# Attention and a one-expert MoE on one core: the last transpose of a query tile is placed behind both heads' scores

## The chip, the cores and the metric

The kernel runs on one core of a Trainium2 chip. The metric is device time in microseconds (us). The kernel before takes 1197.86 us, the median of three runs from 1194.87 to 1198.07. Engines are named as in the profile: PE (TensorE; PEld are its weight loads), DVE (VectorE), ACT (ScalarE), POOL (GpSimd) and SP (SyncE, which here only issues DMAs).

## What is computed

Attention with 8 batches, 8 heads, 576 positions and head size 64, with a bias from a small network on relative positions, and behind it a mixture of experts in which each of the 4608 tokens goes to the one expert with the largest gate.

```python
scores = scale * np.matmul(q, k.transpose(0, 1, 3, 2)) + bias
scores = scores - np.max(scores, axis=-1, keepdims=True)
attn = np.exp(scores)
attn = attn / (np.sum(attn, axis=-1, keepdims=True) + 1e-09)
out = np.matmul(attn, v)                      # per batch and head
...
expert_idx = np.argmax(x @ w_gate, axis=1)
for e in range(E):
    mask = expert_idx == e
    h = np.maximum(x[mask] @ w1[e], 0.0)
    out[mask] = gate_w[mask, None] * (h @ w2[e])
```

## The kernel before

Two heads make a pair, and there are 32 pairs (8 batches of 4). The queries of a pair are cut into five tiles, four of 128 rows and one of 64. The first two pairs run while the bias is built (`attend`); the other thirty go through `attend_units`, which the change touches. There a unit is a pair with its tiles [0, 1] or [2, 3, 4] (the last two pairs have units of one tile), and a step `k` is one query tile.

For one step, `scores` writes the scores of the two heads into two PSUM tiles `s` (four matmuls each, line 165; the pool `ps_s` has two buffers). DVE adds the bias and takes the minimum of the negated scores (line 170), ACT takes the exponential (line 173). The result `a` has 128 queries by 1152 keys, so it needs nine transposes of 128 by 128 on PE before it can be multiplied with the values: `turn` writes four of them (block 0), four (block 1) and one (block 2, the one that holds the end of both heads' keys) into PSUM tiles `tps`. The pool `ps_t` has two buffers, which the blocks take in turn. Block 0 is copied out by ACT (line 216), block 1 by DVE (line 214), block 2 by ACT (line 206). For the 64-row tile the two heads lie side by side: there is no block 1, block 0 is copied by DVE (line 212), and block 2 (line 201) is copied by two ACT copies (line 203).

The steps are overlapped: while the scores of step k are written, blocks 0 and 1 of step k-1 are transposed (`first_turns`), block 2 belongs to step k-2 (`last_turn`), and a number of value products (lines 221 and 224) and output rows (line 234) of an older unit follow. On PE the order is the order in which the program writes these pieces, since each call of `pe` is tied behind the one before. On ACT, DVE, POOL and SP a scheduler sets the order from its own timeline of the whole program.

In one step PE therefore does: scores of head 1; block 2 of step k-2; scores of head 2; blocks 0 and 1 of step k-1; rows and value products. Because the two `tps` buffers alternate, block 1 of step k-1 takes the buffer that block 2 of step k-2 was written to, and has to wait until ACT has copied that out. After a 64-row tile there is no block 1, and so no such wait.

The q and k of a coming pair are loaded by SP into raw tiles (`qn`, `kn`, one buffer), split by ACT (line 139) and DVE (line 140) into a rounded part and a rest, and moved by DMAs of line 144 to `qs`, `k1` and `k2` (two buffers each). Once per batch, `route` ranks the tokens (lines 378 to 427): two small matmuls (lines 398 and 399), a chain of small DVE instructions up to the row numbers `pi` (line 411), and five indirect DMAs on POOL (line 425), which write the rows to DRAM. After attention the experts run (`Experts`), in blocks of up to 384 tokens.

Of the kernel before, what the change touches and what calls it, by code (L numbers as in the profile page):

```python
# [77 lines left out]
def attention(tc, ctx, q, kt, vm, ltab, bcst, gate, gt, cm, cmat, ival, tail0, pcst, bias, xs, plan, moe):  # L78
# [140 lines left out]
    def values(v, at, o, N):  # L219

        yield nc.tensor.matmul(o[:, :N], v[:, 4], at[:, 8, :N], start=True, stop=False, skip_group_check=True)
        for c in range(4):
            for hh in range(2):
                mm = nc.tensor.matmul(o[64 * hh:64 * hh + 64, :N], v[:, c, 64 * hh:64 * hh + 64], at[:, 4 * hh + c, :N], start=False, stop=c == 3, skip_group_check=True)  # L224
                if hh:
                    yield mm

    def rows(b, pr, qts, osb, rl):

        x = ps_x.tile([P, 512], F32, name="x")  # L230
        c0 = 0
        for i, qt in enumerate(qts):
            n = QN[qt]
            mm = nc.tensor.matmul(x[:n, i * XC:(i + 1) * XC], osb[:, c0:c0 + n], gt[:, pr], start=True, stop=True)
            c0 += n
        for i, (qt, r) in enumerate(zip(qts, rl)):
            n = QN[qt]
            if n < P:
                nc.vector.tensor_scalar(out=r[:, :1], in0=r[:, :1], scalar1=1e-9, scalar2=None, op0=ALU.add)
                nc.vector.reciprocal(out=r[:n, 1:2], in_=r[n:2 * n, :1])  # L240
                nc.vector.reciprocal(out=r[:n, :1], in_=r[:n, :1])
            else:
                nc.vector.tensor_scalar(out=r, in0=r, scalar1=1e-9, scalar2=None, op0=ALU.add)
                nc.vector.reciprocal(out=r, in_=r)
            rb = r[:n].rearrange("p (a o) -> p a o", o=1)
            nc.vector.tensor_tensor(out=xsb[b, qt][:n, pr * P:(pr + 1) * P].rearrange("p (a d) -> p a d", a=2),
                                    in0=x[:n, i * XC:i * XC + P].rearrange("p (a d) -> p a d", a=2), in1=rb.broadcast_to([n, 2, D]), op=ALU.mult)
            nc.vector.tensor_tensor(out=lgs[b % 2][:n, qt, pr], in0=x[:n, i * XC + P:(i + 1) * XC].rearrange("p (a e) -> p a e", a=2),
                                    in1=rb.broadcast_to([n, 2, E]), op=ALU.mult)
        return mm  # L250
# [15 lines left out]
    def attend_units(units, ahead, after):  # L266

        steps = [(u, i) for u, (b, pr, qts) in enumerate(units) for i in range(len(qts))]
        state = [{"a": [], "r": [], "N": 0} for _ in units]
        prev = []
        turned, ended, prod = [], [], []

        def pe(f):

            if prev:
                with tc.issue_after(prev[0].ins):
                    prev[:] = [f()]  # L280
            else:
                prev[:] = [f()]

        def finish():
            for u in ended:
                b, pr, qts = units[u]
                pe(lambda: rows(b, pr, qts, state[u]["osb"], state[u]["r"]))
                for qt in qts:
                    after(b, pr, qt)
            ended.clear()  # L290

        def products(count):

            for _ in range(count):
                if not prod:
                    if not turned:
                        return
                    u = turned.pop(0)
                    b, pr, qts = units[u]
                    o = ps_o.tile([P, 512], F32, name="o")  # L300
                    prod[:] = [u, 5, o, values(loaded[b * NPAIR + pr][3], state[u]["at"], o, state[u]["N"])]
                u, left, o, g = prod
                pe(lambda: next(g))
                prod[1] -= 1
                if not prod[1]:
                    prod.clear()
                    N = state[u]["N"]
                    state[u]["osb"] = atp[1].tile([P, atp[2]], F32, name="osb")
                    nc.scalar.copy(out=state[u]["osb"][:, :N], in_=o[:, :N])
                    ended.append(u)  # L310

        def first_turns(u, i):
            st, qts = state[u], units[u][2]
            if i == 0:
                while any("osb" not in st for st in state[:max(u - 1, 0)]):
                    products(1)
                st["at"] = atp[0].tile([P, 9, atp[2]], F32, name="at")
            pe(lambda: turn(st["a"][i], st["at"], QN[qts[i]], st["N"], [0, 1]))

        def last_turn(u, i):  # L320
            st, qts = state[u], units[u][2]
            pe(lambda: turn(st["a"][i], st["at"], QN[qts[i]], st["N"], [2]))
            st["N"] += QN[qts[i]]
            if i == len(qts) - 1:
                turned.append(u)

        extra = []

        def one_more():

            if extra:
                with tc.issue_after(prev[0].ins):
                    if next(extra[0], extra) is extra:
                        extra.clear()

        for k, (u, i) in enumerate(steps):
            b, pr, qts = units[u]
            more = ahead(b, pr, qts[i])
            if more:
                extra[:] = [more]  # L340
            one_more()
            halves = scores(b, pr, qts[i])
            pe(lambda: next(halves)[2])
            if k > 1:
                last_turn(*steps[k - 2])

            def second():
                a, r, mm = next(halves)
                state[u]["a"].append(a)
                state[u]["r"].append(r)  # L350
                return mm
            pe(second)
            if k:
                first_turns(*steps[k - 1])
                finish()
                products(UNIT_STEPS[(k - 1) % QT] if len(units[steps[k - 1][0]][2]) > 1 else 5)
        last_turn(*steps[-2])
        first_turns(*steps[-1])
        one_more()
        finish()  # L360
        products(5)
        one_more()
        last_turn(*steps[-1])
        one_more()
        products(10)
        mm = prev[0]
        finish()
        return mm
# [119 lines left out]
    with ExitStack() as es:  # L488
# [63 lines left out]
        steps = [(0, 0), (0, 1), (1, 0), (1, 1), (2, 0), (2, 1), (3, 0), (4, 0), (3, 1), (4, 1)]  # L552
# [36 lines left out]
    def after(b, pr, qt):  # L589
        advance(1)  # L590
        if pr == NPAIR - 1 and qt == QT - 1:
            pending.append(route(b))
# [312 lines left out]
```

## Time and profile before

| | |
|---|---|
| device time, median of 3 runs | 1197.86 us (1194.87 to 1198.07) |
| the profiled execution | 1203.04 us, of which the span of instructions 1201.3 us |
| mean granted TensorE clock | 0.965 |
| busy share of the span | PE 92%, PEld 74%, DVE 57%, ACT 46%, POOL 14% |
| PE busy from 300 to 450 us | 146.89 of 150 us |

Attention in `attend_units` runs from about 125 to 700 us, the experts from there to the end. The time of a row is its start from the span's start, then its length; a matmul's end is modelled, and matmuls overlap, so the pace of PE is read from the starts of neighbouring rows.

### The profile page before, as it was taken

How to read it: one execution, taken by the hardware profiler on the slowest of the kernel's cores; microseconds unless marked ns; L12 is line 12 of the kernel's file. 1: busy time of each engine (PE TensorE's matmuls, PEld its weight loads, DVE VectorE, ACT ScalarE, POOL GpSimd, SP SyncE). 2: the span in 40 equal slices, each digit the busy share in tenths (PEclk: the TensorE clock that was granted, in tenths of full speed). 3: DMA queues.
4: the chain of work that ended last, by engine and by line, in shares of the span. 5: the costliest groups of instructions: out<-in, count | busy, mean ns of one | idle time of the engine just before them, and what ended most of it. 6: DMA issues, size and time to landing. Idle time of an engine off the chain costs nothing. (4 is left out here: it accounts for less than half of the span.)

```text
span 1201.3 us, 21037 instructions
## 1 busy us (share of the span) xinstructions
PE 1111.0 (92%) x7332; PEld 883.0 (74%) x7332; DVE 680.7 (57%) x2025; ACT 558.3 (46%) x1315; POOL 168.6 (14%) x224
## 2 busy tenths in 40 slices
PE   6699889999999999999999997999989899989893
PEld 2256667777777777777677786998978788978782
DVE  6587667787787878878677763322413222414141
ACT  5587556676667666676566551111302211313130
POOL 0000000101001010010100402400042140032320
PEclk8699989999999999999999999999999999999897
DMA  8845765757658677576565705420251700342400
GB/s 227 191 117 119 186 154 156 208 162 206 164 157 215 160 203 181 153 217 173 174 171 159 229 34 183 187 71 27 71 186 45 251 27 18 102 155 71 168 18 27
DMA packets 70089, 171.85 MB, mean 143 GB/s; under 512 B 11298, under 2 KB 11810, under 8 KB 69794
## 3 DMA queue, kind: packets, MB, share of 16 engines
q1 hardware_dynamic: 63682, 150.07, 45.4%
q0 software_dynamic: 5920, 18.95, 4.3%
q8 instruction: 73, 1.20, 0.4%
q14 instruction: 126, 1.03, 0.3%
q10 hardware_dynamic: 288, 0.59, 0.1%
HBM read 75.00 MB, written 23.97 MB: 82 GB/s over the span
## 5 line engine op out<-in xcount | busy, mean ns | idle before, releaser
L165 PE MATMUL s<-k,qs 128*128 128x288 f32 x1280 | 238.9, 322 | 16.0 <-ACT ob L536 7.8
L173 ACT ACTIVATE a<-t,mn 128x576 f32<-128x576 f32 x288 | 222.7, 774 | 59.8 <-DVE mn L170 49.9
L165 PEld LDWEIGHTS s<-k,qs 128*128 128x128 f32 x1280 | 184.8, 191 | 75.6 <-issue 32.3
L693 PE MATMUL psh<-bias,bias 128*128 128x384 f32 (+2 forms) x1248 | 210.3, 326 | 23.6 <-issue 21.9
L170 DVE CUSTOM_DVE_ANT_0 t<-s,bias 128x576 f32<-128x576 f32 x288 | 210.8, 751 | 33.1 <-PE s L165 29.3
L693 PEld LDWEIGHTS psh<-bias,bias 128*128 128x128 f32 x1248 | 202.3, 198 | 29.8 <-issue 23.7
L210 PE MATMUL tps<-gt,a 128*128 128x128 f32 x1152 | 165.9, 278 | 15.3 <-ACT at L206 7.8
L683 ACT ACTIVATE bias<-psh 128x384 fp32r<-128x384 f32 (+2 forms) x104 | 46.7, 451 | 266.4 <-PE psh L693 266.1
L210 PEld LDWEIGHTS tps<-gt,a 128*128 128x128 f32 x1152 | 131.4, 142 | 35.8 <-ACT at L206 13.1
L224 PE MATMUL o<-at,v 128*64 128x320 f32 (+3 forms) x1216 | 154.3, 379 | 0.0
L684 DVE SCALAR_TENSOR_TENSOR bias<-psh,bias 128x384 fp32r<-128x384 f32 (+2 forms) x104 | 51.7, 504 | 112.2 <-ACT bias L683 111.9
L224 PEld LDWEIGHTS o<-at,v 128*64 128x64 f32 x1216 | 70.6, 136 | 51.2 <-issue 26.3
L214 DVE COPY at<-tps 128x512 f32<-128x512 f32 x128 | 87.9, 687 | 6.1 <-PE tps L210 1.6
L727 PE MATMUL psy<-w2h,bias 128*128 128x512 f32 (+1 forms) x224 | 88.8, 398 | 0.0
L216 ACT COPY at<-tps 128x512 f32<-128x512 f32 x128 | 73.9, 577 | 30.8 <-PE tps L210 30.2
L728 PE MATMUL psy<-w2l,bias 128*128 128x512 f32 (+1 forms) x224 | 88.2, 396 | 0.0
L729 PE MATMUL psy<-w2h,bias 128*128 128x512 f32 (+1 forms) x224 | 87.2, 397 | 0.0
L394 POOL TENSOR_TENSOR cs<-cs,oh 128x8 f32<-128x8 f32 x40 | 8.0, 201 | 512.8 <-DVE oh L389 510.4
L731 DVE TENSOR_SCALAR y<-psy,g 128x512 f32<-128x512 f32 (+1 forms) x38 | 28.4, 748 | 91.0 <-PE psy L729 91.0
L732 POOL DMA_INDIRECT out<-y,ids x38 | 37.2, 980 | 301.5 <-DVE y L731 269.1
L534 PE MATMUL s<-h,bc 128*32 128x288 f32 x576 | 59.2, 469 | 12.2 <-ACT ob L536 10.3
L668 ACT CAST bias<-tps 128x384 fp32r<-128x384 f32 (+2 forms) x60 | 24.9, 461 | 87.8 <-PE tps L666 78.4
(164 smaller groups left out, 1411.2 us busy)
## 6 DMA issues: line engine op xcount, KB each, us to landing
k<-hi SPq DMA_DIRECT2D x128, 160.0 KB, 2.9
k<-kn SPq DMA_DIRECT2D x128, 160.0 KB, 3.8
bias<-in_wl SPq DMA_DIRECT2D x28, 512.0 KB, 3.9
qn<-in_q SPq DMA_DIRECT2D x32, 352.0 KB, 4.1
qs<-hi SPq DMA_DIRECT2D x64, 176.0 KB, 2.9
qs<-qn SPq DMA_DIRECT2D x64, 176.0 KB, 3.2
kn<-in_kt SPq DMA_DIRECT2D x32, 320.0 KB, 4.8
v<-in_vm SPq DMA_DIRECT2D x32, 320.0 KB, 3.3
```

The lines of the kernel that those rows point to most:

```text
L165: return nc.tensor.matmul(s[:, hf, :SH], qs[:, hh, i:i + P], (k1, k2)[second][:, hh, k0 + hf * SH:k0 + hf * SH + SH], start=first, stop=last)
L170: nc.vector.tensor_tensor_reduce(out=t[:m], in0=s[:m, :, :SH], in1=bt.rearrange("p (a c) -> p a c", a=2), op0=ALU.add, op1=ALU.min, scale= ...
L173: nc.scalar.activation(out=a[:m, hh * S:(hh + 1) * S], in_=t[:m].rearrange("p a c -> p (a c)"), func=AF.Exp, bias=mn[:m, hh:hh + 1], scale ...
L210: mm = nc.tensor.transpose(tps[:, c], a[:, k0:k0 + P], ident)
L214: nc.vector.tensor_copy(out=at[:, 4:8, c0:c0 + n], in_=tps)
L216: nc.scalar.copy(out=at[:, :4, c0:c0 + n], in_=tps)
L224: mm = nc.tensor.matmul(o[64 * hh:64 * hh + 64, :N], v[:, c, 64 * hh:64 * hh + 64], at[:, 4 * hh + c, :N], start=False, stop=c == 3, skip_ ...
L534: nc.tensor.matmul(ps[32 * j:32 * j + 32, hf, :SH], w2bd, hs[j][:, hf * SH:(hf + 1) * SH], start=True, stop=True)
L693: nc.tensor.matmul(ps[:, :N], w[c][:, k0:k0 + P], x[kc][:, :N], start=i + kc == 0, stop=i == 2 and kc == KC - 1)
L727: nc.tensor.matmul(ps[:n], a, wh, start=f == 0, stop=False)
L728: nc.tensor.matmul(ps[:n], a, wo, start=False, stop=False)
L729: nc.tensor.matmul(ps[:n], b, wh, start=False, stop=f == FC - 1)
```

## The change

Block 2 of step k-2 is written behind the scores of both heads instead of between them. PE's order in a step becomes: scores of head 1, scores of head 2, block 2 of step k-2, blocks 0 and 1 of step k-1, then as before.

```diff
             halves = scores(b, pr, qts[i])
             pe(lambda: next(halves)[2])
-            if k > 1:
-                last_turn(*steps[k - 2])
 
             def second():
                 a, r, mm = next(halves)
...
             pe(second)
+
+            if k > 1:
+                last_turn(*steps[k - 2])
             if k:
                 first_turns(*steps[k - 1])
                 finish()
```

No instruction is added or removed. On PE, in the step of a 64-row tile, the single transpose (L205) changes its place like this (the difference, - before and + after; `k` are the key tiles, `a` the exponentials, `gt` the identity):

```order
 L165 MATMUL s<-k_2229,qs 128x288 x2
 L165 MATMUL s<-k_2230,qs 128x288 x2
-L205 MATMUL tps<-gt,a 128x128
 L165 MATMUL s<-k_2229,qs 128x288 x2
 L165 MATMUL s<-k_2230,qs 128x288 x2
+L205 MATMUL tps<-gt,a 128x128
 L210 MATMUL tps<-gt,a 128x128 x8
 L224 MATMUL o<-at,v 64x256 x4
```

The transpose now stands directly ahead of the eight, of which the second four take its buffer. The same happens in every step from the third on.

On ACT the copies of `tps` and the exponentials keep their order, apart from a few of the last steps. On DVE and PE the scheduler places the ranking of a batch elsewhere: the two matmuls of lines 398 and 399 go from between the scores of the next step to between the two blocks of four transposes of the step before. On DVE, in the pair behind the end of a batch, before:

```order
L403 TENSOR_TENSOR pos<-x,run_119 128x40
L404 TENSOR_TENSOR run<-x,run_119 128x8
L140 TENSOR_TENSOR kn<-kn,hi 128x640
L407 TENSOR_TENSOR pos<-pos,oh 128x40
L170 ISA t,mn<-s,bias_67 128x576
L170 ISA mn 128x1
L212 COPY at<-tps 128x8x64
L409 TENSOR_REDUCE pf<-pos 128x5
L170 ISA t,mn<-s,bias_68 128x576
L170 ISA mn 128x1
L411 CAST pi<-pf 128x5
```

The same place on DVE after the change (lines behind 352 have a number one higher there, so L412 is the cast that was L411):

```order
L404 TENSOR_TENSOR pos<-x,run_119 128x40
L405 TENSOR_TENSOR run<-x,run_119 128x8
L408 TENSOR_TENSOR pos<-pos,oh 128x40
L214 COPY at<-tps 128x4x128
L410 TENSOR_REDUCE pf<-pos 128x5
L239 TENSOR_SCALAR r<-r 128x1
L412 CAST pi<-pf 128x5
L240 RECIPROCAL r<-r 64x1
L241 RECIPROCAL r<-r 64x1
L170 ISA t,mn<-s,bias_67 128x576
L170 ISA mn 128x1
L140 TENSOR_TENSOR kn<-kn,hi 128x640
```

The cast to the row numbers `pi`, for which the indirect DMAs of line 425 wait, now stands ahead of the split of `kn` (L140); before, it stood behind that and behind two more passes over scores (L170). In the expert blocks the scheduler also interleaves the two products differently in places.

## Rows read from the trace of the kernel before

**Rows 1.** Busy time of each engine in two stretches, one of attention and one of the experts (start:end, length, then each engine's busy us and count; PEclk is the granted clock).

```profile
300.00:450.00 150.00, 146.89 (x1036) 111.52 (x1036) 118.90 (x410) 102.39 (x263) 13.23 (x32) 1.00 0.68 180
...
1000.00:1201.00 201.00, 174.34 (x959) 152.38 (x957) 58.44 (x107) 39.41 (x79) 42.85 (x32) 0.94 0.24 83
```

**Rows 2.** The timeline of one step from 403.7 us: scores of head 1, block 2, scores of head 2, the eight transposes, and ACT's copy of block 2.

```profile
403.76 0.80 PE L165 MATMUL s<-k,qs 128*128 128x288 f32 x4
...
404.40 0.27 PE L205 MATMUL tps<-gt,a 128*128 128x128 f32 x1
...
404.42 0.77 PE L165 MATMUL s<-k,qs 128*128 128x288 f32 x4
...
404.70 0.27 ACT L206 COPY at<-tps 128x128 f32<-128x128 f32 x1 [0.76 <-PE tps L205]
...
405.03 1.03 PE L210 MATMUL tps<-gt,a 128*128 128x128 f32 x8
```

**Rows 3.** PE's timeline at two other places: eight scores in a row with transposes behind (a step of the first pairs), and a single transpose with four directly behind it (the last steps of attention).

```profile
110.72 1.32 PE L165 MATMUL s<-k,qs 128*128 128x288 f32 x8
111.88 0.60 PE L210 MATMUL tps<-gt,a 128*128 128x128 f32 x4
...
701.75 0.30 PE L201 MATMUL tps<-gt,a 128*64 128x128 f32 x1
701.88 0.60 PE L210 MATMUL tps<-gt,a 128*128 128x128 f32 x4
```

**Rows 4.** The timeline of a step in which ACT is late: the split of `qn`, the copy of the value products, the copy of block 2, and the eight transposes, whose second four begin with the weight load at 446.78.

```profile
445.46 0.78 ACT L139 CAST hi<-qn 128x704 fp32r<-128x704 f32 x1 [0.76 <-DMA qn<-in_q]
...
446.15 0.42 ACT L309 COPY osb<-o 128x320 f32<-128x320 f32 x1
...
446.17 1.27 PE L210 MATMUL tps<-gt,a 128*128 128x128 f32 x8
...
446.46 0.27 ACT L206 COPY at<-tps 128x128 f32<-128x128 f32 x1
446.78 0.42 PEld L210 LDWEIGHTS tps<-gt,a 128*128 128x128 f32 x4 [0.26 <-ACT at L206]
```

**Rows 5.** From 125 to 700 us: the copies of block 2 (count: ns min/median/max, first and last start), who waited for L206 (total us, times), and the longest idle times of the L210 transposes caused by L203 (PE and PEld together).

```profile
L206 ACT COPY at<-tps x121: 242/266/273, 126.4 to 699.3; 128x128 f32<-128x128 f32 x121
L203 ACT COPY at<-tps x58: 189/205/213, 130.8 to 663.2; 64x64 f32<-64x64 f32 x58
...
  PEld tps L210: 13.1, 20
  PE tps L210: 7.8, 11
...
  ACT at L203: 8.7, 21
```

**Rows 6.** From 130 to 690 us, who waited for whom (total us, times, longest): the DMA queue of SP, and ACT.

```profile
SPq L144 <- PE s L165: 127.3, 27, 8.1
...
ACT hi L139 <- DMA qs<-hi: 48.1, 27, 2.8
...
ACT hi L139 <- DMA qn<-in_q: 20.8, 20, 3.1
```

**Rows 7.** The timeline of one pair's loads: the second scores of the step with a 64-row tile, the DMAs that follow them, the split of `kn`, the next load of `qn`, and its split.

```profile
411.98 0.78 PE L165 MATMUL s<-k,qs 128*128 128x288 f32 x4
...
412.82 1.28 SPq L144 DMA_DIRECT2D qs<-hi  x2
...
416.43 0.73 ACT L139 CAST hi<-kn 128x640 fp32r<-128x640 f32 x1 [1.66 <-DMA qs<-hi]
...
422.38 0.59 SPq L132 DMA_DIRECT2D qn<-in_q  x1
...
425.97 0.78 ACT L139 CAST hi<-qn 128x704 fp32r<-128x704 f32 x1 [0.26 <-DMA qn<-in_q]
```

**Rows 8.** Two pairs behind the end of a batch. In the first: a ranking instruction on DVE, the scores of head 2 that wait for DVE, the row numbers, the first indirect DMA and the load of `qn`. In the second: the load of `qn`, its split, and the second four transposes.

```profile
436.44 0.19 DVE L407 TENSOR_TENSOR pos<-pos,oh 128x40 f32<-128x40 f32 x1
...
437.36 0.80 PE L165 MATMUL s<-k,qs 128*128 128x288 f32 x4 [0.53 <-DVE mn L170]
...
438.60 0.17 DVE L411 CAST pi<-pf 128x5 int32<-128x5 f32 x1
...
439.55 1.02 POOL L425 DMA_INDIRECT xs<-xrow,pi  x1 [5.73 <-DVE mn L170]
...
440.67 0.59 SPq L132 DMA_DIRECT2D qn<-in_q  x1
...
587.12 1.91 SPq L132 DMA_DIRECT2D qn<-in_q  x1
...
594.29 0.78 ACT L139 CAST hi<-qn 128x704 fp32r<-128x704 f32 x1 [3.15 <-DMA qn<-in_q]
...
595.62 0.93 PE L210 MATMUL tps<-gt,a 128*128 128x128 f32 x4 [2.40 <-ACT at L206]
```

**Rows 9.** The stretch behind that wait (as in Rows 1), and six row matmuls in it and in another pair at the full clock.

```profile
595.85:599.26 3.41, 3.41 (x13) 2.57 (x12) 3.10 (x14) 1.83 (x5) 0.00 (x0) 0.50 0.08 30
...
596.35 1.84 PE L234 MATMUL x<-gt,osb 128*128 128x144 f32 x6
...
409.91 1.04 PE L234 MATMUL x<-gt,osb 128*128 128x144 f32 x6
```

## The prediction

> **What bounds the kernel now.** I read the busy time by stretch first. Between 300 and 450 us PE is busy for 146.89 of 150 us at the full granted clock [rows 1], so in the part that the change touches PE is the pace setter, and a pause of PE is paid unless a later pause shrinks by as much. Then I read the timeline of an ordinary step and followed what releases each piece of PE's work. In it block 2 starts at 404.40, ACT copies it from 404.70, and the eight transposes start at 405.03 and last 1.03 us [rows 2]. One transpose alone lasts 0.27, so their pace is (1.03 - 0.27) / 7 = 0.109 us, and the fifth did not wait: its buffer had been free for half a microsecond. Last I looked for the steps in which it does wait. In the step at 446 us the eight take 1.27 us, because ACT was still busy with the split of `qn` (which had waited for its DMA) and a copy, and came to block 2 only at 446.46 [rows 4].
>
> **PE's own work.** The transpose is moved, so what counts is its price at each place. Scores, transpose, scores, up to the first of the eight: 405.03 - 403.76 = 1.27 us [rows 2]. Eight scores in a row up to the next transpose: 111.88 - 110.72 = 1.16 us [rows 3]. Between the scores it costs 0.11. In a run of transposes it costs 0.109 by the pace, or 0.13 by the last steps (701.75 to 701.88) [rows 3]. I take no difference; the bound is 0.02 us for some 140 steps, +2.8 us.
>
> At the full clock the eight transposes of an ordinary step keep the pace of 0.109 us [rows 1, 2]. The Trainium skill, TensorE: Matmul & The Clock Gate, in Part 4 on PE-mode transpose, says the opposite of what I need: that the full clock does not engage for transposes. By the rows this change costs PE nothing; by that rule a longer run of transposes would bring the low clock, which is the fourth rival below. The trace disagrees so far, with 1.00 over 150 us in which nine transposes stand in nearly every step.
>
> **The new wait.** Block 1 of step k-1 (the fifth of the eight) takes the buffer of block 2. ACT starts its copy 0.30 us after block 2 starts and needs 0.27 [rows 2]; the fifth follows the copy's end by 446.78 - 446.73 = 0.05 [rows 4]. That is 0.62 us from block 2 to the fifth. So far 0.6 us of scores and four transposes covered it. After the change only block 2 and the four stand there, 5 x 0.109 = 0.545. So PE waits 0.075 us even when ACT is idle. If the transpose behind block 2 comes at 0.13, the wait is 0.055.
>
> How many steps: there are 121 copies by L206 and 58 by L203, two for each of 29 tiles of 64 rows [rows 5]. Once per pair only four transposes follow and nothing waits, 29 steps. In 20 steps the fifth waits for L206 already now [rows 5]; there ACT is late on its own account, and moving block 2 changes nothing by itself. That leaves 121 - 29 - 20 = 72 steps: 72 x 0.075 = **+5.4 us** (4.0 to 5.8). Behind a 64-row tile ACT needs two copies of 0.205, so the wait from an idle ACT would be 0.30 + 0.41 + 0.05 - 0.545 = 0.22 us; 21 of these 29 steps wait for L203 now, 8.7 / 21 = 0.41 each, which is more [rows 5]. I take 0 for them; the other 8 could add 1.8.
>
> What is queued behind: on ACT an exponential or the copy of block 0 stands behind the copy of block 2, which starts up to 0.5 us later. Both work on results that come about as late, so I take 0; ACT is busy only 102 of 150 us [rows 1]. No DMA is issued by the moved step.
>
> **A cover that is lost.** In the pair behind the end of a batch, the scores of head 2 wait for DVE (0.53 us at 437.36) [rows 8], and block 2 ran inside that wait. Now it runs behind them: 7 batches x 0.109 = **+0.8 us**.
>
> **What gives it back.** The fifth transposes that wait now do so for a chain of DMAs. The DMA queue waits for scores once per pair (27 times) before it moves `qs`; ACT then sits idle for that DMA (27 times, 48.1 us), and later for the load of `qn` (20 times, 20.8 us) [rows 6]. In one pair: scores until 412.76, DMA at 412.82, split of `kn` at 416.43, load of `qn` at 422.38, its split at 425.97 [rows 7]; behind that split on ACT stands the copy of block 2 [rows 4]. The length of this chain does not depend on PE. After the change the scores that start it end 0.11 earlier, because block 2 no longer runs ahead of half of them, and PE arrives later by two new waits of 0.075. Seen from PE the chain ends 0.11 + 0.15 = 0.26 us earlier, and a wait shrinks by that or vanishes. The 20 waits are 13.1 us, 0.65 each [rows 5], as PEld shows them; at 446.78 it shows 0.26 where the eight took 1.27 - 1.03 = 0.24 longer than usual [rows 2, 4], so nearly all of it is PE's, and most waits can give the full 0.26. I take 18 x 0.24 = **-4.3 us**; the bounds are 0 (the chain moves along with PE) and 20 x 0.26 = -5.2.
>
> **The ranking.** The row numbers of a batch come earlier on DVE: the instruction at 436.44 stood behind the split of `kn` and the cast at 438.60 [rows 8]; now both stand ahead of that split and of the pass over scores before it. That is at least 438.60 - 436.44 = 2.2 us, and with the split and the pass (0.8 us each) nearer to 4. So far the five indirect DMAs start at 439.55, about a microsecond ahead of the load of `qn` at 440.67, and compete with it. In the worst pair that load is issued at 587.12 and its split starts at 594.29, 7.2 us later, against 3.6 us in [rows 7], and PE stands for 2.40 us [rows 8]. With earlier indirect DMAs the overlap is smaller, but it doesn't vanish, and the moves to `k` meet them instead. Bounds: 0 and -4 us (the 2.40 and the next largest of the visible gaps, which are 7.8 us for 11 [rows 5], so at most 5.4 for the other ten); I take **-1.5 us**. The ranking instruction of 0.19 us that leaves the way of the waiting scores [rows 8] is worth at most 7 x 0.19 = 1.3 us, and other small ones are put ahead of copies elsewhere; I take 0 with that as a bound either way. In the experts the same matmuls run in another order. PE has 201 - 174 = 27 us of pauses there in the last 201 [rows 1], and no row says that these move; 0, with 2 us either way.
>
> **Sum.** 5.4 + 0.8 - 4.3 - 1.5 = +0.4 us on the profiled execution of 1203.04, so 1203.4. That execution lies 5.2 us above the median of 1197.86; referred to the median the time is **1198.3 us**. About 0.3%, 3.6 us, is what a measurement of this kernel can tell from no change, so this is a forecast of no visible change.
>
> **Rivals.**
> First, slower: the chain of loads doesn't stay where it is but moves along with PE, because each of its links waits for PE or for an ACT that PE feeds. Then nothing is given back and the ranking brings nothing: 5.4 + 0.8 = +6.2, 1204.1 us. For it speaks that the chain starts at scores of PE; against it, that ACT sits idle for its DMAs in every pair [rows 6]. It decides if the give-back stays under about 2.5 us.
>
> Second, faster: the earlier indirect DMAs free the load of `qn`, both long gaps go, and with them the dip of the clock: behind the 2.40 us gap the clock is 0.50 for 3.41 us, and six row matmuls take 1.84 instead of 1.04 us [rows 8, 9], so the dip costs 3.41 x (1 - 1.04 / 1.84) = 1.5 us. With the full give-back: 5.4 + 0.8 - 5.2 - 4 - 1.5 = -4.5, 1193.4 us.
>
> Third, the change doesn't do what it says for the step: ACT is so late that it hides the whole new wait in most steps. The order on ACT doesn't allow it in the 72 steps, since ACT starts the copy as soon as block 2 ends there. Without the 5.4 the sum would be -5.0, 1192.9 us; I count it into the second's chance.
>
> Fourth, the clock: short pauses in most steps and runs of nine transposes bring PE to 1.2 GHz. The nearest row is the dip above; one per pair would be 28 x 1.5 = 42 us, 1240 us. Against it: the stretch at 1.00 already holds waits such as those at 437 and 446 us [rows 1, 4, 8], and the dip followed a pause of 2.40 us [rows 8, 9], not one of 0.1. The Trainium skill, same page, in the section on psum-queue depth-cycling, describes such a clock, falling and rising as PE pauses briefly between groups that cycle through PSUM banks; no stretch of [rows 1] shows it.
>
> **How the numbers follow.** Forecast 0.54, first rival 0.24, second 0.20, fourth 0.02. The range goes from the second to a little above the first: 1193 to 1205 us. Below 1194.3 it is faster: 0.20. Above 1201.5 it is slower: 0.26, the first and the fourth. Between them 0.54.
>
> **What the profile after will show.** The rows of eight transposes that last 1.03 now should last about 1.11 (1.10 to 1.12) in ordinary steps, with the fifth's weight load waiting for L206; that settles the new wait. The waits for L206 in the steps behind a late `qn` should be some 0.25 us shorter; if they are not, the give-back is wrong. The indirect DMAs should start 2 to 5 us earlier against the load of `qn`, and the gaps over 1 us should be fewer. The granted clock should stay at 1.00 between 300 and 450 us. I am wrong if the fifth doesn't wait, if the eight transposes take over 1.2 us in ordinary steps, or if the experts' part differs by more than 2 us.

## The result, and the profile after

The changed kernel takes 1208.43 us in the median of 11 runs (1204.07 to 1213.04), the kernel before, measured beside it, 1195.01 us in 11 runs (1193.22 to 1202.57): a ratio of 1.0094, with an interval of 1.0071 to 1.0116. It is slower by about 0.9%; the forecast was no visible change, 1198.3 us, and its range ended at 1205.

The two profiled executions hide most of this: 1203.04 us before and 1204.26 us after. The one before lies 8.0 us above the median of its kernel, the one after 4.2 us below its own. So they are compared by stage. The 26 pairs from the sixth move of `qs` to the last take 486.4 us before and 492.0 after, what follows 543.8 and 545.9. Ahead of them the trace of before loses 6.6 us (the sixth move starts at 171.1 us there, at 164.5 after): PE stands for 3.08 us there, and a stretch of low clock follows, which the trace after lacks.

In the kernel before, the transposes behind that pause, from PE's timeline, and the busy time of the engines in the stretch around them (columns as in [rows 1]):

```profile
163.00 2.37 PE L210 MATMUL tps<-gt,a 128*128 128x128 f32 x8 [3.08 <-ACT at L216]
...
162.00:169.00 7.00, 5.86 (x22) 4.62 (x22) 4.11 (x16) 4.31 (x12) 0.00 (x0) 0.53 0.17 52
```

The same stages after as in [rows 1]:

```profile
300.00:450.00 150.00, 146.63 (x1023) 109.43 (x1023) 118.17 (x399) 101.22 (x258) 13.65 (x32) 1.00 0.66 179
1000.00:1201.00 201.00, 173.68 (x968) 151.52 (x966) 58.84 (x108) 39.67 (x80) 42.71 (x32) 0.96 0.25 83
```

The clock is still 1.00 in attention, and in the experts PE's pauses are about as long as before. PE looks as busy as before; the busy share doesn't show the loss.

The timeline of an ordinary step after, to be read against [rows 2]: eight scores, block 2, the eight transposes, and the weight load with which the second four begin.

```profile
402.68 1.32 PE L165 MATMUL s<-k,qs 128*128 128x288 f32 x8
403.84 0.27 PE L205 MATMUL tps<-gt,a 128*128 128x128 f32 x1
403.95 1.18 PE L210 MATMUL tps<-gt,a 128*128 128x128 f32 x8
404.15 0.27 ACT L206 COPY at<-tps 128x128 f32<-128x128 f32 x1 [0.81 <-PE tps L205]
404.47 0.42 PEld L210 LDWEIGHTS tps<-gt,a 128*128 128x128 f32 x4 [0.16 <-ACT at L206]
```

The new wait is there: 1.18 us where it was 1.03. The waits from 130 to 690 us (total us, times, longest), to be read against [rows 5, 6]:

```profile
ACT hi L139 <- DMA qs<-hi: 41.4, 28, 2.3
PEld tps L210 <- ACT at L206: 26.8, 80, 2.9
ACT hi L139 <- DMA qn<-in_q: 26.1, 18, 3.5
PE tps L210 <- ACT at L206: 13.3, 9, 2.7
```

The 20 waits for L206 have become 80. But the long ones have not become shorter, as the give-back would have it: those that stop PE visibly went from 7.8 to 13.3 us. Six of these nine, 10.0 us in all, stand in the six pairs that hold a ranking. One of them, by the timeline: the cast of the row numbers, the first indirect DMA, the last four moves to `k`, the load of `qn`, four transposes, the split of `qn`, the copy of block 2, the other four.

```profile
503.63 0.17 DVE L412 CAST pi<-pf 128x5 int32<-128x5 f32 x1
...
504.59 1.01 POOL L426 DMA_INDIRECT xs<-xrow,pi  x1 [2.33 <-DVE r L241]
...
508.19 4.11 SPq L144 DMA_DIRECT2D k<-kn  x4
...
512.34 1.31 SPq L132 DMA_DIRECT2D qn<-in_q  x1
...
516.38 0.60 PE L210 MATMUL tps<-gt,a 128*128 128x128 f32 x4
...
518.32 0.78 ACT L139 CAST hi<-qn 128x704 fp32r<-128x704 f32 x1 [3.54 <-DMA qn<-in_q]
...
519.32 0.27 ACT L206 COPY at<-tps 128x128 f32<-128x128 f32 x1
...
519.64 0.66 PE L210 MATMUL tps<-gt,a 128*128 128x128 f32 x4 [2.66 <-ACT at L206]
```

The same moves to `k` in the kernel before, in the pair of [rows 8]:

```profile
438.17 2.46 SPq L144 DMA_DIRECT2D k<-kn  x4
```

The indirect DMAs start 512.34 - 504.59 = 7.8 us ahead of the load of `qn`, 1.1 before (439.55, 440.67 in [rows 8]). So they now run beside the four moves to `k`, whose issue takes 4.11 instead of 2.46 us. The load of `qn` is queued behind these moves on SP, comes later, and PE stands for 2.66 us. The six ranking pairs of the stretch have a pause of over 1 us at this place, all of them; before it was two of six.

### The profile page after: what moved, and what is told of

Its sections match the earlier page's. It is cut to its first block, busy times and chain, and to the rows that moved or that the text cites. A ratio compares the mean times of both kernels' runs of the same rounds, so it can differ in the third digit from the quotient of the medians.

```text
span 1202.4 us, 21050 instructions
## 1 busy us (share of the span) xinstructions
PE 1109.8 (92%) x7332; PEld 876.0 (73%) x7332; DVE 685.5 (57%) x2025; ACT 561.5 (47%) x1315; POOL 170.9 (14%) x224
## 3 DMA queue, kind: packets, MB, share of 16 engines
q14 instruction: 127, 1.04, 0.3%
## 5 line engine op out<-in xcount | busy, mean ns | idle before, releaser
L165 PE MATMUL s<-k,qs 128*128 128x288 f32 x1280 | 222.1, 313 | 14.2 <-ACT ob L537 7.6
L170 DVE CUSTOM_DVE_ANT_0 t<-s,bias 128x576 f32<-128x576 f32 x288 | 210.2, 751 | 41.9 <-PE s L165 37.8
L165 PEld LDWEIGHTS s<-k,qs 128*128 128x128 f32 x1280 | 179.5, 190 | 73.1 <-issue 24.1
L694 PEld LDWEIGHTS psh<-bias,bias 128*128 128x128 f32 x1248 | 199.6, 195 | 33.0 <-issue 24.3
L210 PE MATMUL tps<-gt,a 128*128 128x128 f32 x1152 | 173.7, 279 | 18.1 <-ACT at L206 13.6
L210 PEld LDWEIGHTS tps<-gt,a 128*128 128x128 f32 x1152 | 128.2, 141 | 46.7 <-ACT at L206 27.7
L214 DVE COPY at<-tps 128x512 f32<-128x512 f32 x128 | 88.1, 688 | 13.4 <-PE tps L210 11.7
L206 ACT COPY at<-tps 128x128 f32<-128x128 f32 x128 | 33.8, 264 | 77.9 <-PE tps L205 77.6
```

Source lines behind the costliest of these rows:

```text
L165: return nc.tensor.matmul(s[:, hf, :SH], qs[:, hh, i:i + P], (k1, k2)[second][:, hh, k0 + hf * SH:k0 + hf * SH + SH], start=first, stop=last)
L170: nc.vector.tensor_tensor_reduce(out=t[:m], in0=s[:m, :, :SH], in1=bt.rearrange("p (a c) -> p a c", a=2), op0=ALU.add, op1=ALU.min, scale= ...
L210: mm = nc.tensor.transpose(tps[:, c], a[:, k0:k0 + P], ident)
L214: nc.vector.tensor_copy(out=at[:, 4:8, c0:c0 + n], in_=tps)
L694: nc.tensor.matmul(ps[:, :N], w[c][:, k0:k0 + P], x[kc][:, :N], start=i + kc == 0, stop=i == 2 and kc == KC - 1)
```

## The experiments

Three theories. **A**: the loss comes from the early indirect DMAs in the ranking pairs. **B**: it is the new wait in ordinary steps. **C**, formed after the first runs, says how A reaches PE: `qn` comes late, ACT stands at its split, the copy of block 2 stands behind the split on ACT, and the fifth transpose behind that copy.

All ratios are to the kernel before, measured beside it. The last two columns are the mean time from one move `qs<-qn` on the DMA queue to the same move of the next pair, between 165 and 645 us of the one profiled execution: 19 or 20 pairs without a ranking, 6 with one. They are left out for the four kernels in which every pair is much longer.

```
kernel               ratio   interval            pair   ranking pair
before               1                           18.33  19.98
after                1.0094  1.0071 to 1.0116    18.36  20.81
before_early         1.0086  1.0056 to 1.0115    18.28  21.74
before_tie           0.9984  0.9963 to 1.0004    18.37  19.60
after_tie            1.0039  1.0017 to 1.0062    18.45  20.89
after_late           1.0041  1.0024 to 1.0057    18.39  21.11
after_spare          1.2187  1.2151 to 1.2223
after_x              0.9993  0.9978 to 1.0009    18.35  19.94
after_x_tie          1.0014  0.9997 to 1.0030    18.09  19.40
before_early_x       1.0174  1.0142 to 1.0205    19.05  20.93
first                1.0044  1.0028 to 1.0060    18.23  20.72
first_tie            0.9934  0.9913 to 0.9955    18.34  18.93
first_late           0.9916  0.9893 to 0.9939    18.34  19.60
after_split          1.2100  1.2068 to 1.2133
before_early_split   1.1833  1.1810 to 1.1857
first_tie_split      1.1568  1.1546 to 1.1590
after_behind         0.9987  0.9975 to 0.9999    18.39  18.90
before_early_behind  0.9932  0.9915 to 0.9948    18.20  18.88
first_tie_behind     0.9795  0.9776 to 0.9813    17.78  18.16
before_behind        0.9892  0.9875 to 0.9909    18.05  19.90
```

The pair columns already speak: the change leaves the pairs without a ranking as they were (18.33, 18.36) and lengthens the others. In the diffs below, `...` marks what is left out.

**The early ranking alone, and its delay.** `before_early` leaves block 2 where it was and only puts the two ranking matmuls between the fours of transposes, with the DVE steps behind them (`hook` holds the ranking until it is called):

```diff
-            pe(lambda: turn(st["a"][i], st["at"], QN[qts[i]], st["N"], [0, 1]))
+            pe(lambda: turn(st["a"][i], st["at"], QN[qts[i]], st["N"], [0]))
+            if hook and k % QT == 4:
+                pe(lambda: hook.pop()())
+            if QN[qts[i]] == P:
+                pe(lambda: turn(st["a"][i], st["at"], QN[qts[i]], st["N"], [1]))
...
```

The `_tie` kernels delay the cast behind the newest scaling of logits on DVE (`newest` holds that instruction):

```diff
...
+        yield
         pi = rp_.tile([P, QT], I32, name="pi")
-        nc.vector.tensor_copy(out=pi, in_=pf)
+        with tc.issue_after(newest[0].ins):
+            nc.vector.tensor_copy(out=pi, in_=pf)
```

> The kernel before, with block 2 at its old place between the scores of both heads, but with the ranking of a batch put where the change brings it: its two matmuls between the two fours of transposes, its DVE steps and the cast of pi ahead of the split of kn. So the indirect DMAs should start as early as in the changed kernel, and no new wait is there. Theory A: 6 to 9 us slower than the kernel before, 1201 to 1204, with moves to k that take over 4 us in ranking pairs and gaps of 1 to 3 us ahead of the fifth transpose there. Theory B: within 3 us of the kernel before, 1192 to 1198.

> The kernel before, with the same delay of the cast of pi and nothing else. It prices the delay by itself. In the kernel before the indirect DMAs start about 1 us ahead of the load of qn already; a stage later they start beside or behind it. Theory A: the start of the indirect DMAs matters, so this may go either way by a few us, within 4 us of the kernel before (1191 to 1199). Theory B: the start of the indirect DMAs doesn't matter: within 1.5 us of the kernel before.

> The changed kernel, with one thing undone: the cast of the row numbers pi, on which the indirect DMAs of a batch wait, stands one stage later and behind the newest score scaling on DVE, so the indirect DMAs should start about as late in the pair as before the change (about 1 us ahead of the load of qn, not 4 to 5 us ahead of it). PE's order is that of the changed kernel. Theory A (most of the loss, 6 to 9 us, comes from the six or seven ranking pairs, whose indirect DMAs now meet the moves to k; the new wait is nearly given back): 1199 to 1203 us, some 6 to 9 us under the changed kernel, and the gaps of over 1 us between the fourth and the fifth transpose go. Theory B (the new wait in ordinary steps, 72 x 0.14 = 10 us, is the loss and is not given back): 1207 to 1210 us, no visible change against the changed kernel.

> The kernel after_tie with the cast of pi one more stage later, so the indirect DMAs start some 4 us later still, about when the load of qn has landed (13 us behind the move of qs instead of 9). Theory C: the split of qn in the ranking pairs starts like in other pairs, 12 us behind the move of qs; the ranking pairs fall from 20.9 to under 19.5 us and the ratio to the kernel before from 1.004 to 0.998 to 1.002. If the 0.4% that after_tie kept are not from its ranking pairs, it stays at 1.003 to 1.005.

`before_early` is slower by 0.86%, nearly the whole loss of the change without its move (A expected 6 to 9 us; 1.0086 is 10). Its timeline in one ranking pair, in the order of the rows after:

```profile
512.65 1.01 POOL L434 DMA_INDIRECT xs<-xrow,pi  x1 [2.33 <-DVE r L242]
...
516.38 3.96 SPq L144 DMA_DIRECT2D k<-kn  x4
...
520.38 1.31 SPq L132 DMA_DIRECT2D qn<-in_q  x1
...
526.63 0.78 ACT L139 CAST hi<-qn 128x704 fp32r<-128x704 f32 x1 [2.89 <-DMA qn<-in_q]
...
527.95 0.33 PE L211 MATMUL tps<-gt,a 128*128 128x128 f32 x1 [2.61 <-ACT at L207]
```

It is the picture of the changed kernel: moves of 3.96 us, a late `qn`, a pause of 2.61 us. One thing more differs: in its six ranking pairs the scheduler puts the copy of block 0 behind the next exponential on ACT, which it does neither before nor after the change. Over the six ranking pairs the four moves take 2.47 us on average before, 4.35 in `before_early`, 4.38 after and 2.46 in `after_tie`; the split of `qn` starts 13.7, 15.0, 14.7 and 12.5 us behind the move of `qs`. So A holds in this order: the early ranking is enough for a loss of this size.

In the kernel before, the delay by itself changes nothing clear (`before_tie`, 0.9984). In the changed kernel it gave back only 1.0094 to 1.0039, though, and `after_late`, whose further stage moved no instruction (its order is that of `after_tie`), repeats that with 1.0041. In `after_tie` the load comes in time, but the ranking pairs still last 20.9 us. There the scheduler also put the split of `qn` ahead of one exponential more on ACT. In three of the six pairs PE stands for about 2 us. In two of these pauses ACT and DVE both stand, and the profile names no engine of the core as the releaser ("remote"). One of them:

```profile
443.80 0.27 PE L206 MATMUL tps<-gt,a 128*128 128x128 f32 x1
...
444.18 0.90 POOL L429 DMA_INDIRECT xs<-xrow,pi  x1 [0.30 <-issue]
...
446.21 0.76 DVE L171 CUSTOM_DVE_ANT_0 t<-s,bias 128x576 f32<-128x576 f32 x1 [1.55 <-remote]
446.25 0.27 ACT L207 COPY at<-tps 128x128 f32<-128x128 f32 x1 [2.28 <-remote]
...
446.57 0.65 PE L211 MATMUL tps<-gt,a 128*128 128x128 f32 x4 [2.06 <-ACT at L207]
```

Both wait for results of PE that its records put 2 us earlier, and the fifth indirect DMA is issued just then. What holds them is open.

**The wait taken away by another buffer.** `after_spare` writes block 2 into unused columns of the newest score tile, the `_x` kernels into the tile `x`:

```diff
-            tps = ps_t.tile([P, 4, P], F32, name="tps")
+            tps = newest[0][:, :1, 512 - P:] if blk == 2 and newest else ps_t.tile([P, 4, P], F32, name="tps")
```

```diff
-            tps = ps_t.tile([P, 4, P], F32, name="tps")
+            tps = ps_x.tile([P, 512], F32, name="x").rearrange("p (c q) -> p c q", c=4) if blk == 2 else ps_t.tile([P, 4, P], F32, name="tps")
```

> The changed kernel, with block 2 written to columns of the newest score tile that no score uses, so it takes none of the two transpose buffers and the fifth transpose needn't wait for the copy of block 2. The early ranking stays. What it brings instead is that the copy of block 2 holds the score buffer a little longer. Theory A: little is won, 0 to 4 us, 1204 to 1208, and the gaps of over 1 us in ranking pairs stay in some form. Theory B: 8 to 12 us faster than the changed kernel, 1196 to 1200. In both the eight transposes of an ordinary step should last 1.03 us again.

> The changed kernel, with block 2 written to the accumulator tile x (free in those steps) instead of one of the two transpose buffers, so the fifth transpose no longer waits for the copy of block 2 (L206); the early ranking stays. The eight transposes of an ordinary step should last 1.03 us again instead of 1.17 to 1.19. If the early ranking is the larger cost (theory A: the last call gave +0.86% for it alone), this stays 0.3 to 0.8% slower than the kernel before, with gaps of over 1 us and moves to k of over 4 us in the ranking pairs. If the new wait is the cost (theory B), it is within 0.2% of the kernel before or faster.

> The same, with the cast of pi delayed as in the run after_tie: neither the new wait nor the early indirect DMAs are left, only the order of the scores and transposes. Both theories: faster than after_tie by the new wait, 52 ordinary steps x 0.139 = 7 us less what the chain of DMAs gives back; so a ratio to the kernel before of 0.995 to 1.000. If it stays at 1.004 as after_tie, the wait costs nothing and the order itself does.

> The kernel before_early (early ranking in the order of before, +0.86%), with block 2 written to the tile x, so that the fifth transpose no longer waits for the copy of block 2. The moves to k should still take over 4 us in the ranking pairs and the split of qn still start 14 to 16 us after the move of qs. Theory C (the early indirect DMAs delay qn, ACT stands at its split, the copy of block 2 stands behind the split on ACT, and the fifth transpose behind that copy): without the last link the pairs with a ranking fall from 21.7 to about 20 us, and the kernel is within 0.3% of the kernel before. If it stays at 1.006 or more, the delay reaches TensorE by another way and theory C is wrong.

`after_spare` says nothing of the theories: block 2 now waits until DVE has read the scores of that tile (130 to 690 us; total us, times, longest):

```profile
PE s L208 <- DVE mn L171: 106.8, 81, 2.9
```

`after_x` looked like a win for B: no wait, the eight in 1.04 us, no loss, and the indirect DMAs early. Its moves to `k` still take over 4 us in most ranking pairs (3.5 to 4.8), yet these pairs last 19.9 us:

```profile
402.08 1.04 PE L210 MATMUL tps<-gt,a 128*128 128x128 f32 x8
402.28 0.27 ACT L206 COPY at<-x 128x128 f32<-128x128 f32 x1 [0.89 <-PE x L205]
```

That is how C came about: with this buffer the fifth transpose waits for no copy behind the split, be it an ordinary or a late one. But the tile `x` has readers of its own, and in `before_early_x` block 2 waits for them in every pair:

```profile
PE x L206 <- DVE r L244: 23.6, 28, 1.8
```

There the pairs without a ranking grew too, from 18.28 to 19.05 us. So that run missed its expectation (1.0174, where 1.006 was to speak against C), `after_x_tie` came out just above its own (1.0014, not 0.995 to 1.000), and the `_x` runs can't tell the theories apart.

**Block 2 ahead of both heads.** `first` moves the same transpose the other way, with 1.2 us of scores between it and the fifth; `first_late` has the order of `first_tie`.

```diff
             halves = scores(b, pr, qts[i])
+            if k > 1:
+                last_turn(*steps[k - 2])
             pe(lambda: next(halves)[2])
...
             pe(second)
-
-            if k > 1:
-                last_turn(*steps[k - 2])
```

> The kernel with block 2 ahead of the scores of both heads instead of behind them: scores of both heads in a row, as in the changed kernel, but 1.2 us of scores cover the copy of block 2, so the fifth does not wait. The ranking is early here too. Theory A: 0.4 to 0.9% slower than the kernel before, by the early indirect DMAs alone. Theory B: within 0.2% of the kernel before.

> The same as first, with the cast of pi delayed. Theory A: 0.4 to 0.8% faster than first, so within 0.3% of the kernel before. Theory B: the same as first within 0.2%.

> The kernel first_tie (0.9934, faster than both) with the same further delay. If the indirect DMAs still cost something there, it is 0.1 to 0.4% faster than first_tie, 0.989 to 0.993. If first_tie's gain is its order of scores and transposes, the same within 0.1%.

Here, where the new wait is not added, the ranking is early too and costs 1.1 to 1.3%: 1.0044 with it, 0.9934 and 0.9916 without. The ranking pairs, 20.72 against 18.93 and 19.60 us, carry most of it. But the last link is another one than in C: in the six ranking pairs of `first` the copy of block 2 already stands ahead of the split, and what PE waits for is the copy of block 0, which stands behind the split and an exponential. Block 2 of the next step takes its buffer. One such pause by the timeline, and all of them from 130 to 690 us:

```profile
514.12 0.33 PE L205 MATMUL tps<-gt,a 128*128 128x128 f32 x1 [2.50 <-ACT at L216]
...
PE tps L205 <- ACT at L216: 12.2, 6, 2.5
```

Two runs of one order lie 0.002 apart; so much must be allowed between ratios measured at different times.

**The split of `qn` behind the copy of block 2.** The `_split` kernels wrote the splits and their moves three steps later in the program (first diff), the `_behind` kernels only tie the split of `qn` behind the third newest copy of block 2, which is the one of the step it falls in (second):

```diff
...
             if qt == 1:
-                load_qk(*divmod(u, NPAIR))
+                splits[:] = [load_qk(*divmod(u, NPAIR), later=u < total - 1)]
+                next(splits[0], None)
...
+            elif qt == 4 and splits:
+                list(splits.pop())
```

```diff
+            if src is qn and len(copied) > 3:
+                with tc.issue_after(copied[-3].ins):
+                    nc.scalar.copy(out=hi, in_=src)
+            else:
+                nc.scalar.copy(out=hi, in_=src)
-            nc.scalar.copy(out=hi, in_=src)
```

> The changed kernel with only the place of the split of qn moved: on ACT it now stands behind the copy of block 2 instead of ahead of it, so a late load of qn can no longer hold that copy, and with it the fifth transpose. The early indirect DMAs and the new wait in ordinary steps stay; the DMA queue's order is unchanged. Theory C (the loss of the change runs through the split of qn on ACT, in the ranking pairs): moves to k still over 4 us, but the ranking pairs fall from 20.8 to 19.0 to 19.8 us and the ratio to the kernel before from 1.009 to 0.997 to 1.003. Theory B (the loss is the new wait): 1.006 to 1.010, as the changed kernel.

> The same move of the split of qn in before_early (order of before, early ranking, +0.86%). Theory C: the ranking pairs fall from 21.7 to 19.0 to 20.0 us and the ratio from 1.0086 to 0.997 to 1.003. If the early ranking costs by another way than the split of qn on ACT, it stays at 1.006 or more.

> The fastest so far (first_tie, 0.9934 and 0.9916) with the split of qn behind the copy of block 2 too. Theory C: a little more is won, since its fifth transposes still wait up to 1.3 us for that copy, 14 us in all on the weight load: 0.986 to 0.991. If the split's new place only moves the wait to the next move of qs, 0.992 to 0.996.

The three `_split` runs are misses of the edit: the moves had been running a pair ahead, and now come when the scores need them (`after_split`, 130 to 690 us):

```profile
PE s L174 <- DMA k<-kn: 67.5, 22, 5.8
PE s L174 <- DMA k<-hi: 59.2, 15, 7.6
```

> The changed kernel with the split of qn on ACT behind the copy of block 2 of the same step instead of ahead of it, and nothing else moved by a step or a pair (the run after_split had put the split and all moves behind it a pair later, so that scores waited for k). Theory C: the moves to k still take over 4 us in the ranking pairs and the split still comes at 14 to 15 us, but no fifth transpose waits for it; the ranking pairs fall from 20.8 to 19.0 to 20.0 us and the ratio to the kernel before from 1.009 to 0.997 to 1.003. Theory B (the new wait in ordinary steps is the loss): 1.006 to 1.010. If the exponential and the copy of block 0, which now stand behind the split, stop TensorE instead, the pauses of over 1 us move to the values or to the first transpose of the next step, and it stays over 1.004.

> The same in before_early (order of before, early ranking, 1.0086). Theory C: ranking pairs from 21.7 to 19.0 to 20.0 us, ratio 0.997 to 1.003. Otherwise it stays over 1.004.

> The same in first_tie (0.9934 and, in a second run of the same order, 0.9916). Theory C: its 14 us of waits of the fifth for the copy of block 2 fall to under 6 us, ratio 0.985 to 0.991. Otherwise 0.990 to 0.996.

> The kernel before, with only the split of qn behind the copy of block 2 on ACT; the indirect DMAs stay as late as in the kernel before. Beside before_early_behind (0.9932) it prices the early indirect DMAs once the way through the split is cut, and beside after_behind (0.9987) the move by itself. Theory C: the early indirect DMAs then cost nothing, so 0.990 to 0.996, and the pairs without a ranking last 18.0 us. If it is faster than 0.989, they still cost by another way.

These test C directly. In `after_behind` the indirect DMAs are early, the moves to `k` long and the new wait in place, as the rows show:

```profile
499.42 1.02 POOL L432 DMA_INDIRECT xs<-xrow,pi  x1 [1.82 <-DVE pi L418]
...
503.94 4.22 SPq L150 DMA_DIRECT2D k<-kn  x4
...
508.20 0.61 SPq L134 DMA_DIRECT2D qn<-in_q  x1
...
511.84 1.18 PE L216 MATMUL tps<-gt,a 128*128 128x128 f32 x8
...
512.04 0.27 ACT L212 COPY at<-tps 128x128 f32<-128x128 f32 x1 [0.93 <-PE tps L211]
512.20 0.78 ACT L143 CAST hi<-qn 128x704 fp32r<-128x704 f32 x1
```

Against the changed kernel, ACT's order has the split behind the copy of block 2 and the copy of block 0 behind one exponential more; DVE's half of the split moves along, a few small instructions of DVE and POOL are placed elsewhere, and the order of SP's DMAs, and of PE in these pairs, is the same. The copy no longer waits for the split, the eight last 1.18 us where they were held up for 2.66, the ranking pairs fall from 20.81 to 18.90 us, and the whole from 1.0094 to 0.9987. The waits of the transposes for that copy, from 130 to 690 us:

```profile
PEld tps L216 <- ACT at L212: 14.8, 82, 1.5
PE tps L216 <- ACT at L212: 1.8, 3, 1.3
```

82 waits where the changed kernel has 80, but 1.8 us of those that stop PE visibly, where there were 13.3. `before_early_behind` does the same for the order of before (1.0086 to 0.9932, faster than expected; ranking pairs 21.74 to 18.88). For the long pauses of the ranking pairs C is so shown from both sides: the early ranking alone brings them, and reordering split and copy takes them away.

For the whole kernel it is less sharp, because the kernel before gains as much by the same edit: `before_behind` stands at 0.9892, mainly in its pairs without a ranking (18.33 to 18.05), where late copies cost something too. With the split out of the way in both kernels, the change still costs 0.9987 / 0.9892 = 1.0096, from ratios measured at different times. So the loss of the change as a whole is not shown to run through the split alone.

Part of what is left is the move itself, now that no late copy hides it: 0.9987 / 0.9932 = 1.0055, measured side by side. There the new wait, theory B, is paid: pairs without a ranking last 18.39 instead of 18.20 us. `after_tie` against `before_tie` gives 1.0055 as well, but in its ranking pairs (20.89, 19.60) and by the open pauses above. `before_behind` is 0.4% below `before_early_behind`, while its ranking pairs are longer (19.90, 18.88); whether early indirect DMAs still cost something when the split is out of the way stays open. `first_tie_behind` beats both kernels, by 2.05% against the one before.

## Why the prediction was wrong, point by point

The lengths of the five steps of a pair show most terms at once (medians of 19 to 27 steps of all pairs, without the steps that hold ranking matmuls; from the start of the scores to the next; a step is named by the transposes and products that follow):

```
step                        before  after  before_behind  after_behind
eight, 8 products           3.339   3.479  3.339          3.479
four, 8 products            2.812   2.818  2.812          2.818
64-row block 2, eight       4.457   4.250  4.446          4.249
eight, 12 products          4.013   4.135  4.013          4.143
eight, rows, 2 products     3.719   3.605  3.477          3.604
sum                         18.340  18.287 18.087         18.293
```

**PE's own work**: right. In the step without a new wait the moved transpose costs 0.006 us.

**The new wait**: right in kind, sized too small. There are 80 waits for L206, where 72 new ones and 20 old ones were counted. The fifth follows block 2 after 404.47 - 403.84 = 0.63 us, forecast 0.62. But behind the wait the transposes don't fall back into their pace at once: the second four last 0.66 instead of 0.60 us (519.64 and 516.38 in the rows after). So a step pays 0.12 to 0.14 us, not 0.075; 72 steps would be 10 us, not 5.4.

**The lost cover**: not found. The two steps behind a batch's end take 6.56 us in both traces, the new wait of one of them included.

**The give-back**: as large as the new waits, but mostly by another way than I named. Pairs without a ranking are no longer than before (18.33, 18.36). The named part is smaller than forecast: the last step of the table waited 0.24 us for a late copy (3.719 against 3.477 in `before_behind`); that wait goes and the new one takes its place, so the step gains 0.11 (3.719 to 3.605), not 0.24. The other part I had set to 0: in the 64-row step the moved transpose fills a pause that PE had ahead of the eight, and the wait for L203 shrinks. In the kernel before:

```profile
418.80 0.42 PEld L210 LDWEIGHTS tps<-gt,a 128*128 128x128 f32 x4 [0.21 <-issue]
...
419.60 0.42 PEld L210 LDWEIGHTS tps<-gt,a 128*128 128x128 f32 x4 [0.38 <-ACT at L203]
```

and after:

```profile
413.85 0.42 PEld L210 LDWEIGHTS tps<-gt,a 128*128 128x128 f32 x4
...
414.52 0.42 PEld L210 LDWEIGHTS tps<-gt,a 128*128 128x128 f32 x4 [0.25 <-ACT at L203]
```

That is about 0.2 us in each pair (4.457 to 4.250).

**The ranking** is the step that failed. I took -1.5 us, with bounds of 0 and -4: earlier indirect DMAs would overlap less with the load of `qn`. They do start earlier, 7.8 instead of 1.1 us ahead of it. My own sentence said that the moves to `k` meet them instead, and then priced that at nothing, though the load of `qn` is queued behind these moves on SP. The sign was wrong: `before_early` measures +0.86%, 10 us, for the early ranking in the order of before, and the ranking pairs of the changed kernel are 0.8 us longer on average, 7 x 0.8 = 6 us. The six of before hold one of 22.8 us, the pair of [rows 8] with the 2.40 us; the other five average 19.4, and against these alone the difference is 1.4 us, 7 x 1.4 = 10 us. Whether so slow a pair is usual in the kernel before, one trace can't tell. The bound should have reached to the loss that [rows 8] already show: a late `qn` costs 2.40 us, and seven pairs could pay that.

**The experts** are unchanged: from the last row matmul of attention (L234) to the end 489.9 us before, 490.2 after. The 2 us more behind the last move of `qs` stand in the last steps of attention, in which the seventh ranking's indirect DMAs run.

**The rivals.** The first, slower, has the sign but not the reason: it holds that nothing is given back, and the pairs without a ranking show that the new waits were. Its time, 1204.1, is nearer by luck. The second saw the same late `qn` and took the wrong side. The third didn't come: the new wait stands in the rows. The fourth, the clock, didn't come: 1.00 through waits in three of five steps. The Trainium skill, TensorE: Matmul & The Clock Gate, Part 4, says that the full clock does not engage for transposes; the row of 300 to 450 us after, at 1.00 with nine in a row in most steps, still doesn't agree. What transposes alone would be granted it can't tell, since other matmuls run in every step. In [rows 1] attention is at 1.00, but the experts are at 0.94; that no stretch shows a falling clock holds for attention alone.

**The announced signs.** Eight transposes in 1.17 to 1.18 us, not 1.10 to 1.12; indirect DMAs earlier by 6.6 us, not 2 to 5; in the ranking pairs more gaps over 1 us, not fewer, and the waits behind a late `qn` there not 0.25 us shorter but longer. None of the three things that were to show me wrong (no wait of the fifth, eight transposes over 1.2 us, other experts) came: none of them looked at the ranking.

Of the 13.4 us between the medians, the two traces place 5 us in the six ranking pairs (6 x 0.83) and 2 behind them. `before_early` makes it likely that the ranking takes more than that, about 10; the rest I can't place, since the traces are single executions.

## What to carry to other kernels

When the written order of one engine changes, follow what else the scheduler moves with it: a ranking that no line of this change touches cost 0.86% by itself (`before_early`), because DMAs that start earlier ran beside another queue's moves, and a load was waiting behind these. Where a short copy on which the bottleneck waits is queued behind an instruction that waits for a load, reorder these two first: in the kernel before that alone was worth 1.1%, and it decides what other changes seem to cost. The move costs next to nothing on top of the early ranking while late copies hide it (1.0094 / 1.0086), and 0.55% when they don't.

## What the runs showed of the hardware that I had not expected

Four moves of 64 rows took about 2.46 us to issue in all six ranking pairs of the kernel before, and 4.1 to 4.7 us in all six after the change, beside indirect DMAs in flight (4.11, 3.96 and 4.22 in the rows). Behind a semaphore wait, four transposes took 0.66 us instead of 0.60, after 2.66 us as after 0.16 (403.95 + 1.18 - 404.47 in the ordinary step). And a pause of 2.66 us was followed by a stretch at half the clock, as in [rows 9], where pauses of 0.16 us in most steps were not:

```profile
520.84:524.26 3.42, 3.42 (x13) 2.84 (x14) 2.04 (x10) 1.58 (x4) 0.00 (x0) 0.50 0.00 0
```
